# Pooled attention with a SoLU layer on one core: the first batch's scores in float32, q turned tile by tile on TensorE, and a new order of the program

## The chip, the core and the metric

The kernel runs on one core of one Trainium2 chip. What counts is the time of one execution on the device in microseconds (us). The engines are TensorE (PE in the profile; PEld is its weight load), VectorE (DVE), ScalarE (ACT), GpSimd (POOL) and SyncE (SP), which here only issues transfers. Each engine has its own queue and works through it in order; semaphores tie the queues together.

## The reference

```
B, H, S, D = 8, 8, 576, 64                          # q, k, v: float32
k_p = k.reshape(B, H, 72, 8, D).mean(axis=3)        # pooled by 8; v the same
scores = q @ k_p.T / sqrt(D)                        # per batch and head: 576 x 72
attn = softmax(scores)
x = (attn @ v_p)  -> (B * S, H * D) = (4608, 512)
h = x @ w_in                                        # 512 x 1024
solu = h * softmax(h)
ln = (solu - mean) / sqrt(var + 1e-06) * g_ln
out = ln @ w_out                                    # 1024 x 512
```

The weights lie in memory as 64-bit floats (4 MB each), so the kernel has to put float32 words together before it can use them.

## The kernel before

The 4608 tokens are cut into 36 tiles of 128 rows: four of a batch (rows 0 to 511), then one "mix" tile with the last 64 rows of two batches, then four of the next batch. A tile runs through scores (`scores`, L751, tile name `sc`), maximum and subtraction on VectorE (L762, L765), exponential on ScalarE (L772), sum, reciprocal and product on VectorE (L776 to L791, tile `e`), a split of `e` into two float16 parts (`e16`: ScalarE L813 and L815, GpSimd), a transposing DMA (`eT`), the product with v (`e_rest`, L841, tile `xp`), a split of x (`xT`: L849 on ScalarE, L853 on VectorE), the first layer (`mm1`, L873, tile `hp`, 24 matmuls of 512 columns), SoLU and norm on all engines, and the second layer (`op`, L1005).

A product of float32 is done as three passes over float16 parts, high times high and the two mixed ones. So scores need q and k in high and low parts. For q that is a maximum over the batch (`amx_q`, L348), a spread over the partitions on PE (`gq`), a power-of-two scale from it (L370 to L382), the high part (`q_hi`, L722, ScalarE), the low part (`q_lo`, L727, VectorE), and a transposing DMA on SP's queue (`q_T`, L739, tile `qT`). For the first batch's k: GpSimd pools it in adds by halves (`pool_kv`, L329), ScalarE doubles it (`k_two`, L387), PE turns it (`k_T`, L396, tile `kTp`), ScalarE and VectorE make the parts (L412, L421).

Before `hp` of tile 0 can start, the four pieces of w_in must be ready, and this is a chain of its own. A piece is loaded (`w_load`; the raw tiles are `wo` for pieces 0 and 1, whose place it borrows, and `wir2`, `wir3`), its exponent field is brought into place (`w_exp`, L512, ScalarE; `u_wi`), words are joined on VectorE (L524, L545), the largest absolute value is taken (`w_abs`, L535, ScalarE; `ab_wi`), and from all four comes one scale (`g_wi`, L553 to L577). Only then follow, for each piece, the high part (`w_hi`, L645, ScalarE, 1024 columns), on PE the residue (`w_res`: two float32 matmuls L666 against a scaled identity `dg` made at L659, each followed by a subtraction L669; tile `res_wi`, in the two PSUM buffers of `ps_h` that `hp` uses as well), and the low part from it (`w_lo`, L675, ScalarE).

The order is not a scheduler's: `ORDER` is a table of operation numbers, the program is issued in that order (`tc.manual_schedule`), and so it sets the sequence of every engine's queue, SP's with its loads and transposing DMAs among them. Pools with a fixed number of buffers (`raw8` and `raw4` for raw loads, `ps_s`, `ps_x`, `ps_h` in PSUM) add waits.

## Time and profile before

| | |
|---|---|
| Median of 3 runs | 480.9 us (480.87 to 481.13) |
| Span of the profiled execution | 478.6 us |
| Busy: PE, DVE, ACT, POOL | 444.0, 341.3, 354.1, 349.8 us |
| Chain that ended last, by engine | PE 82%, DMA 6%, DVE 5%, ACT 4% |

The span is what the profile covers of its execution. The profiled execution's own time outside the profiler is not recorded, so the profile stands beside the timed runs by its span: 2.3 us less than their median. A line name such as L666 is a line of the kernel before; `x16` is a number of instructions; `<-` says what ended an engine's wait.

### The profile page before, as it was taken

To read this page: it belongs to the slowest core of one execution; us is meant where nothing else is said; L and a number is where in the kernel's file an instruction comes from. 1 tells how busy PE (TensorE), PEld (TensorE's weight loads), DVE (VectorE), ACT (ScalarE), POOL (GpSimd) and SP (SyncE) were. 2 spreads that over 40 slices of the span, in tenths; PEclk is the share of its full clock that TensorE was granted. 3 is DMA by queue.
4 is the path that set the end of the run, shared out by engine and by line. 5 is a ranking of instruction groups with operands and counts; after the bars stand their busy time and mean duration, and the time that the engine had idled before them with its cause. 6 is when DMAs were issued, how large, how long until landed. Compare 5 with 4: busy or idle time off the path is not lost.

```text
span 478.6 us, 9046 instructions
## 1 busy us (share of the span) xinstructions
PE 444.0 (93%) x3100; PEld 230.5 (48%) x3100; DVE 341.3 (71%) x835; ACT 354.1 (74%) x593; POOL 349.8 (73%) x489
## 2 busy tenths in 40 slices
PE   0177999999999999999999999999999999999996
PEld 0033544555455555555545554555545554545462
DVE  2989998599668876677668976787657887783620
ACT  1789999769876687767876698677766688766751
POOL 6256789968999987997989568996999538535340
PEclk9999999999999999999999999999999999999999
DMA  8999864999889889899878888889997648436351
GB/s 259 417 347 214 229 120 109 186 227 235 192 213 195 219 184 216 177 209 205 202 164 198 186 205 169 205 174 209 205 208 165 150 101 144 113 86 147 74 136 59
DMA packets 201390, 89.14 MB, mean 186 GB/s; under 512 B 177664, under 2 KB 186112, under 8 KB 200832
## 3 DMA queue, kind: packets, MB, share of 16 engines
q1 hardware_dynamic: 201344, 88.57, 78.9%
q8 instruction: 24, 0.39, 0.4%
q14 instruction: 22, 0.18, 0.1%
HBM read 36.70 MB, written 9.44 MB: 96 GB/s over the span
## 4 chain that ended last, share of the span: by engine, by line
PE 82%; DMA 6%; DVE 5%; ACT 4%; issue 1%; SPq 1%; POOL 0%; ACTq 0%; POOLq 0%
PE op L1005 36%; PE hp L873 36%; PE xp L841 6%; DMA qT<-q 4%; PE sc L751 3%; DMA qr<-in_q_dram 2%; DVE wo L677 1%; DVE m L883 1%; DMA zT<-z 1%; DVE u_wo L524 0%; ACT xT L849 0%; ACT osb L1013 0%; ACT q L722 0%; ACT sc L772 0%; ACT ab_wo L535 0%
## 5 line engine op out<-in xcount | busy, mean ns | idle before, releaser
L1005 PE MATMUL op<-wo,zT 128*128 128x512 f16 (+1 forms) x888 | 197.3, 373 | 1.2 <-DMA zT<-z 0.7
L873 PE MATMUL hp<-wi,xT 128*128 128x512 f16 x864 | 195.8, 379 | 2.6 <-ACT xT L849 2.6
L873 PEld LDWEIGHTS <-xT 128*128 128x128 f16 x864 | 82.7, 98 | 97.8 <-ACT xT L849 3.2
L1005 PEld LDWEIGHTS <-zT 128*128 128x128 f16 x888 | 84.4, 98 | 91.8 <-DMA zT<-z 1.7
L940 POOL TENSOR_TENSOR z<-z,z 128x512 f16<-128x512 f32 x71 | 82.2, 1168 | 43.3 <-ACT z L927 40.9
L883 DVE TENSOR_REDUCE m<-hp 128x1 f32<-128x1024 f32 x36 | 44.0, 1223 | 28.3 <-PE hp L873 28.2
L820 POOL TENSOR_TENSOR e<-e,e 128x512 f16<-128x512 f32 x36 | 41.6, 1156 | 22.2 <-ACT e L813 22.0
L329 POOL TENSOR_TENSOR vr<-vr 128x512 f32<-128x512 f32 (+3 forms) x48 | 48.1, 1006 | 13.3 <-DMA vr<-in_v_dram 12.7
L932 ACT ACTIVATE z<-z,sz 128x1024 f16<-128x1024 f32 x36 | 41.2, 1145 | 17.1 <-DVE z L918 16.9
L894 ACT ACTIVATE z<-hp,nb,Hb 128x1024 f32<-128x1024 f32 x32 | 38.3, 1198 | 15.2 <-DVE nb L886 14.2
L918 DVE SCALAR_TENSOR_TENSOR z<-hp,rs,z 128x1024 f32<-128x1024 f32 x36 | 46.1, 1280 | 3.4 <-ACT z L894 2.0
L329 POOL TENSOR_TENSOR kr<-kr 128x512 f32<-128x512 f32 (+3 forms) x48 | 42.2, 889 | 2.9 <-DMA kr<-in_k_dram 2.3
L762 DVE TENSOR_REDUCE mx<-sc 128x8 f32<-128x576 f32 x36 | 27.2, 754 | 23.6 <-PE sc L751 23.4
L927 ACT ACTIVATE z<-z,sz 128x1024 f32<-128x1024 f32 x36 | 41.1, 1143 | 0.7
L841 PEld LDWEIGHTS <-vb 128*128 128x128 f16 x640 | 35.3, 98 | 8.2 <-DMA eT<-e 0.4
L1013 ACT ACTIVATE osb<-op,f 128x512 f32<-128x512 f32 (+1 forms) x37 | 24.7, 666 | 19.2 <-PE op L1005 11.9
L841 PE MATMUL xp<-eT,vb 128*128 128x128 f16 (+1 forms) x640 | 38.2, 214 | 0.0
L953 ACT ACTIVATE junk<-z 128x1024 f16<-128x1024 f32 x36 | 37.7, 1047 | 0.2
L732 POOL TENSOR_TENSOR q<-qr,q 128x512 f16<-128x512 f32 x28 | 32.3, 1156 | 7.2 <-ACT q L722 7.2
L776 DVE TENSOR_REDUCE sc<-sc 128x8 f32<-128x576 f32 x36 | 27.4, 762 | 13.5 <-ACT sc L772 13.3
L849 ACT ACTIVATE xT<-xp 128x512 f16<-128x512 f32 x36 | 21.3, 591 | 16.0 <-PE xp L841 15.7
L853 DVE SCALAR_TENSOR_TENSOR xT<-xp,xT 128x512 f16<-128x512 f32 x36 | 24.5, 681 | 6.2 <-ACT xT L849 6.1
(232 smaller groups left out, 588.2 us busy)
## 6 DMA issues: line engine op xcount, KB each, us to landing
kr<-in_k_dram SPq DMA_DIRECT2D x16, 512.0 KB, 4.3
qr<-in_q_dram SPq DMA_DIRECT2D x16, 512.0 KB, 4.9
vr<-in_v_dram SPq DMA_DIRECT2D x16, 512.0 KB, 4.8
out_dram<-osb SPq DMA_DIRECT2D x31, 256.0 KB, 3.0
wor<-in_moe_w_out_dram SPq DMA_DIRECT2D x4, 1024.0 KB, 9.2
wo<-in_moe_w_in_dram SPq DMA_DIRECT2D x2, 1024.0 KB, 7.9
wir<-in_moe_w_in_dram SPq DMA_DIRECT2D x2, 1024.0 KB, 11.9
out_dram<-osb SPq DMA_DIRECT2D x10, 128.0 KB, 2.3
```

Of the source, the lines that this page charges most:

```text
L329: nc.gpsimd.tensor_tensor(out=dst, in0=src[:, :, :n], in1=src[:, :, n : 2 * n], op=ALU.add)
L820: nc.gpsimd.tensor_tensor(out=m[:, 1], in0=e_pair(i)[:, :, :P], in1=m[:, 0], op=ALU.subtract)
L841: nc.tensor.matmul(xp[:, c, lo:hi], lhsT=vb[b % 2][:, x, c].rearrange("p j d -> p (j d)"), rhs=eT[:, e, lo:hi], start=(n == 0), stop=(n == 3),
L873: nc.tensor.matmul(hp[:, f], lhsT=xT[:, xt, c], rhs=wi[:, wt, c, f * 512 : (f + 1) * 512], start=(part == 0 and n == 0), stop=(part == 2 a ...
L883: nc.vector.tensor_reduce(out=small(i, "m"), in_=tl[i]["hp"], axis=AX.XY, op=ALU.max)
L894: nc.scalar.activation(z, t["hp"], AF.Exp, bias=t["nb"], scale=hsc(i, 0), accum_out=small(i, "se"))
L918: nc.vector.scalar_tensor_tensor(out=t["z"], in0=t["hp"], scalar=t["rs"], in1=t["z"], op0=ALU.mult, op1=ALU.mult, accum_out=small(i, "sz"),)
L927: nc.scalar.activation(t["zf"], t["zf"], AF.Identity, bias=t["sz"], scale=-float(DFF))
L932: nc.scalar.activation(t["z16"][:, 0], t["zf"], AF.Identity, bias=t["sz"], scale=-float(DFF))
L940: eng.tensor_tensor(out=t["z16"][:, 1, fs], in0=t["zf"][:, fs], in1=t["z16"][:, 0, fs], op=ALU.subtract)
L953: nc.scalar.activation(junk, t["zf"], AF.Square, scale=DFF**-0.5, accum_out=small(i, "V"))
L1005: nc.tensor.matmul(op_, lhsT=zT[:, zt, c], rhs=wo[:, wt, c, cols(hf)], start=(part == 0 and n == 0), stop=(part == 2 and n == len(todo) - 1),)
```

## The change

The first four tiles (`FULL`) get their scores another way. q of batch 0 is loaded in four pieces, one per tile (`load_q0`, runs of 256 bytes). PE turns a piece by four float32 transposes into PSUM (`q_turn`), ScalarE copies it to SBUF in float32 (`q_keep`), and PE takes the scores as four float32 matmuls of 144 columns against `kd`, which holds the turned pooled k in float32 as blocks of two heads over 128 rows with zeros beside them (`k_zero` on VectorE, two copies `k_put` on ScalarE). So for these tiles maximum, scale, parts and transposing DMA of q fall away, and the exponential's scale is the constant 1/64 (`s_exp`). Batch 0's k is pooled by VectorE, not GpSimd. The float16 form of its k is still needed, by the mix tile, and is made later, in the way of the other batches. The scores of tiles 1 and 2 lie in `ps_h` (`ASIDE`), not in `ps_s`. The first loads of batch 1's k and v go to `raw4`. The whole order is new.

```
 ORDER = (
-    2, 0, 1, 12, 3, 4, 11, 50, 5, 6, 56, 57, 7, 53, 8, 58, 54, 13, 182, 51, 52, 9, 183, 55, 75, 65,
+    0, 52, 2, 58, 53, 59, 54, 60, 1, 55, 56, 57, 61, 69, 3, 189, 4, 13, 82, 11, 76, 12, 7, 5,
...
-        if b == 0:
+        if b < 2:
             return ("raw4", which, b, part)
...
+    def load_q0(eng, i):
+        if "q" not in bat[0]:
+            bat[0]["q"] = p2.tile([P, 4, H, D], F32, tag="qr", name="qr0")
+        rows = q[0, :, :SA, :].rearrange("h (p s) d -> s p h d", s=4)[i]
+        eng.dma_start(bat[0]["q"][:, i], rows)
...
-        nc.gpsimd.tensor_tensor(
-            out=dst, in0=src[:, :, :n], in1=src[:, :, n : 2 * n], op=ALU.add
-        )
+        eng = nc.vector if (b, which) == (0, "kr") else nc.gpsimd
+        eng.tensor_tensor(out=dst, in0=src[:, :, :n], in1=src[:, :, n : 2 * n], op=ALU.add)
...
+    def k_zero():
+        t = p2.tile([P, 2 * NC, P], F16, tag="eT", name="kd")
+        bat[0]["kd"] = t.rearrange("p c n -> p (c n)").bitcast(F32)[:, :NR]
+        nc.vector.memset(bat[0]["kd"], 0.0)
+
+    def k_put(j):
+        r_ = slice(64 * j, 64 * j + 64)
+        nc.scalar.activation(
+            bat[0]["kd"][r_].rearrange("p (c e r) -> p c e r", e=2, r=SP)[:, :, j],
+            bat[0]["kTp"][r_, :NR].rearrange("p (c e r) -> p c e r", e=2, r=SP)[:, :, j], AF.Copy,
+        )
...
-    DIRECT = (0, 1, 2, 3)
+    FULL = (0, 1, 2, 3)
+    ASIDE = (1, 2)
...
+    def q_turn(i):
+        t = ps_x.tile([P, HB, P], F32, tag="x", name=f"qTp{i}")
+        turned[i] = t
+        for c in range(HB):
+            nc.tensor.transpose(
+                t[:, c], bat[0]["q"][:, i, 2 * c : 2 * c + 2].rearrange("p h d -> p (h d)"), ident
+            )
+
+    def q_keep(i):
+        t = p2.tile([P, H, P], F16, tag="qT", name=f"qT{i}")
+        t = t.rearrange("p h n -> p (h n)").bitcast(F32).rearrange("p (c n) -> p c n", n=P)
+        nc.scalar.activation(t, turned[i], AF.Copy)
+        turned[i] = t
...
+        if i in FULL:
+            for c in range(HB):
+                nc.tensor.matmul(
+                    sc[:, c // 2, (c % 2) * PR : (c % 2 + 1) * PR], lhsT=turned[i][:, c],
+                    rhs=bat[0]["kd"][:, c * PR : (c + 1) * PR], start=True, stop=True,
+                )
+            return
...
-        nc.scalar.activation(sc, sc, AF.Exp, scale=grp["ct", q_key(i)])
+        ct = 1.0 / 64 if i in FULL else grp["ct", q_key(i)]
+        nc.scalar.activation(sc, sc, AF.Exp, scale=ct)
```

Three places of the order carry the argument. The first is SP's queue from the program's start. A row says the line, the tile that is written, the memory it is read from, and the shape. Before:

```order
L598 DMA g_sb_107<-in_moe_g_ln_dram 128x8x1
L305 DMA qr0_141<-in_q_dram 128x4x256 x2
L295 DMA vr0_2_144<-in_v_dram 16x2x512 x2
L501 DMA wo_89<-in_moe_w_in_dram 128x2048 x2
L501 DMA wir2_152<-in_moe_w_in_dram 128x2048
L501 DMA wir3_155<-in_moe_w_in_dram 128x2048
L501 DMA wor0_159<-in_moe_w_out_dram 128x2x1024
L292 DMA vr0_0_164<-in_v_dram 128x2x512
L739 DMA_TRANSPOSE qT0_208<-q16_0_195 128x8x128
L292 DMA vr0_1_216<-in_v_dram 128x2x512
L501 DMA wor3_219<-in_moe_w_out_dram 128x2x1024
L739 DMA_TRANSPOSE qT1_224<-q16_1_206 128x8x128
```

After, with the line numbers of the changed kernel:

```order
L321 DMA qr0_152<-in_q_dram 128x8x64 x2
L302 DMA vr0_2_160<-in_v_dram 16x2x512 x2
L299 DMA vr0_0_164<-in_v_dram 128x2x512
L299 DMA vr0_1_167<-in_v_dram 128x2x512
L516 DMA wo_89<-in_moe_w_in_dram 128x2048
L321 DMA qr0_152<-in_q_dram 128x8x64
L516 DMA wo_89<-in_moe_w_in_dram 128x2048
L516 DMA wir2_196<-in_moe_w_in_dram 128x2048
L516 DMA wir3_224<-in_moe_w_in_dram 128x2048
L321 DMA qr0_152<-in_q_dram 128x8x64
L516 DMA wor3_248<-in_moe_w_out_dram 128x2x1024
L516 DMA wor0_280<-in_moe_w_out_dram 128x2x1024
```

The transposing DMAs of q (`qT0`, `qT1`) are gone. v's two pieces `vr0_0` and `vr0_1` stand ahead of the four loads of w_in (`wo` twice, `wir2`, `wir3`), q's third piece among them, and `g_sb` has gone to a later place. Behind the rows shown follow three loads of batch 1's k, two of `qm0`, `wor1`, `wor2` and then `eT0`, the first transposing DMA on the queue; before, `eT0` stood behind `qT1`, `wor1`, `qm0`, `wor2`, the small last piece of batch 1's k, `qT2` and two small loads of v.

The second is ScalarE's queue between the weights' exponents and the first piece's high part, `w_hi`. Before:

```order
L535 ACTIVATE ab_wi1_231,bnd_wi_221<-u_wi1_214 128x1024
L512 ACTIVATE u_wi3_235<-wir3_155 128x1024
L535 ACTIVATE ab_wi2_237,bnd_wi_221<-u_wi2_228 128x1024
L535 ACTIVATE ab_wi3_241,bnd_wi_221<-u_wi3_235 128x1024
L512 ACTIVATE u_wo0_245<-wor0_159 128x1024
L722 ACTIVATE q16_2_264<-qr0_141,sq('b', 0)_178 128x8x64
L659 ACTIVATE dg_wi0_284<-ident_103,sw_wi_257 128x128
L645 ACTIVATE wi_88<-wir3_155,sw_wi_257 128x1024
```

After:

```order
L431 ACTIVATE vp_0_92<-vp_0_92,sv0_264 128x384
L849 ACTIVATE e16_1_97<-e1_269 128x2x32
L472 ACTIVATE vr_99<-vp_0_92 32x128
L550 ACTIVATE ab_wi3_294,bnd_wi_252<-u_wi3_261 128x1024
L847 ACTIVATE e16_1_97<-e1_269 128x512
L755 ACTIVATE qT3_304<-qTp3_299 128x512
L472 ACTIVATE vr_99<-vp_0_92 32x128
L849 ACTIVATE e16_0_96<-e0_240 128x2x32
L469 ACTIVATE v2_0_308<-vp_0_92 128x256
L849 ACTIVATE e16_1_97<-e1_269 128x2x32
L527 ACTIVATE u_wo0_337<-wor0_280 128x1024
L660 ACTIVATE wi_88<-wir2_196,sw_wi_330 128x1024
```

Between the last `ab_wi` (the maxima) and the first write to `wi_88` stood the exponents of w_out's first piece (`u_wo0`), a part of q and `dg`; now seven rows stand there, `u_wo0` among them and six of the split of `e`, of q's last copy and of v. `dg` now follows `w_hi`.

The third is PE's queue ahead of the first layer of tile 0. Before, matmul rows alone, and of each group the first (a residue has four rows, scores and `xp` 16):

```order
L357 MATMUL gv0_344<-identb_105,amx_v_101 128x128
L666 MATMUL res_wi0_346<-wo_89,dg_wi0_284 128x512
...
L666 MATMUL res_wi1_373<-wo_89,dg_wi0_284 128x512
...
L357 MATMUL gq('m', 0)_394<-identb_105,amx_q_102 128x128
...
L751 MATMUL sc2_407<-kT0_211,qT2_321 128x72
...
L666 MATMUL res_wi2_427<-wir2_152,dg_wi0_284 128x512
...
L841 MATMUL xp0_446<-eT0_368,vb_0_94 128x128
...
L873 MATMUL hp0_471<-wi_88,xT0_466 128x512
```

After:

```order
L369 MATMUL g_wi_320<-identb_105,g1_wi_297 128x128
L775 MATMUL sc3_344<-kd_150,qT3_304 128x144 x4
L681 MATMUL res_wi2_364<-wir2_196,dg_wi0_351 128x512
...
L369 MATMUL gq('m', 0)_375<-identb_105,amx_q_102 128x128
L681 MATMUL res_wi3_401<-wir3_224,dg_wi0_351 128x512
...
L369 MATMUL gk1_410<-identb_105,amx_k_100 128x128
L681 MATMUL res_wi1_413<-wo_89,dg_wi0_351 128x512
...
L875 MATMUL xp0_426<-eT0_394,vb_0_94 128x128
...
L681 MATMUL res_wi0_471<-wo_89,dg_wi0_351 128x512
...
L907 MATMUL hp0_476<-wi_88,xT0_458 128x512
```

The scores of tile 2 stood between residues, those of tile 3 behind the first 16 matmuls of `hp0`; now the scores of all four tiles stand ahead of the first residue. The residue of the piece that is last has moved behind `xp0`, directly ahead of `hp0`.

## Rows read from the trace of the kernel before

**Rows 1.** The trace in stretches; busy us by engine, granted clock, DMA share, GB/s
```profile
26.00:32.00 6.00, 5.78 (x23) 2.43 (x22) 5.43 (x15) 4.69 (x7) 4.80 (x6) 1.00 1.08 390
60.00:440.00 380.00, 378.44 (x2707) 196.31 (x2705) 283.02 (x696) 291.90 (x499) 304.82 (x415) 1.00 0.81 178
```

**Rows 2.** The chain of waits, first 60 us: shares by line
```profile
by line: DMA qT<-q 33.9%; DMA qr<-in_q_dram 12.8%; PE hp L873 8.9%; DVE u_wo L524 3.9%; ACT q L722 3.5%; issue 3.4%; ACT ab_wo L535 2.7%; DVE sc L765 2.4%; DVE mx L762 2.4%; ACT e L813 2.1%; DVE m L883 2.0%; DVE amx_q L348 2.0%; SPq L297 1.
```

**Rows 3.** The timeline, PE at the first layer of tiles 0 and 1
```profile
45.81 3.63 PE L873 MATMUL hp<-wi,xT 128*128 128x512 f16 x16 [1.48 <-ACT xT L849]
53.51 1.90 PE L873 MATMUL hp<-wi,xT 128*128 128x512 f16 x8 [0.81 <-ACT xT L849]
```

**Rows 4.** The timeline, the first work on k
```profile
10.29 0.86 POOL L329 TENSOR_TENSOR kp<-kr 128x128 f32<-128x128 f32 x2
11.19 0.74 ACT L387 ACTIVATE k<-kp 128x640 f32<-128x640 f32 x1 [9.11 <-POOL kp L329]
13.58 1.35 PE L396 MATMUL kTp<-ident,k 128*128 128x128 f32 x5
```

**Rows 5.** The timeline, ScalarE from the first q part on, and the first residue
```profile
14.07 0.72 ACT L722 ACTIVATE q<-qr,sq('b', 0)_178 128x512 f16<-128x512 f32 x1 [2.15 <-DVE sq('b', 0)_178 L382]
24.99 1.10 ACT L512 ACTIVATE u_wo<-wor 128x1024 f32<-128x1024 f32 x1
27.09 0.39 ACT L659 ACTIVATE dg_wi<-ident,sw_wi 128x128 f32<-128x128 f32 x1
27.38 1.20 ACT L645 ACTIVATE wi<-wir,sw_wi 128x1024 f16<-128x1024 f32 x1
27.53 2.07 PE L666 MATMUL res_wi<-wir,dg_wi 128*128 128x512 f32 x2
```

**Rows 6.** The timeline, three groups of PE matmuls
```profile
26.48 1.14 PE L751 MATMUL sc<-kT,qT 128*128 128x72 f16 x16 [0.21 <-DMA qT<-q]
32.51 0.68 PE L751 MATMUL sc<-kT,qT 128*128 128x72 f16 x16 [0.35 <-ACT wi L645]
36.57 1.06 PE L666 MATMUL res_wi<-wo,dg_wi 128*128 128x512 f32 x2
```

**Rows 7.** Groups by line and form, first 60 us: count, busy, mean ns, idle before
```profile
L772 ACT ACTIVATE sc<-sc,ct('b', 0)_203 128x576 f32<-128x576 f32 x4 | 2.8, 706 | 1.7 <-DVE sc L765 1.7
L813 ACT ACTIVATE e<-e 128x512 f16<-128x512 f32 x4 | 2.5, 621 | 0.0
L815 ACT ACTIVATE e<-e 128x64 f16<-128x64 f32 x8 | 1.9, 245 | 0.0
L849 ACT ACTIVATE xT<-xp 128x512 f16<-128x512 f32 x3 | 1.7, 583 | 0.0
L791 DVE TENSOR_TENSOR e<-sc,r 128x576 f32<-128x576 f32 x4 | 3.0, 748 | 0.0
```

**Rows 8.** The timeline, ScalarE from v's scaling to a low part
```profile
37.48 0.61 ACT L407 ACTIVATE vp<-vp,sv 128x384 f32<-128x384 f32 x1
39.10 1.00 ACT L675 ACTIVATE wi<-res_wi 128x1024 f16<-128x1024 f32 x1
```

**Rows 9.** k of batch 0, loads: issues (ns, first and last start) and landing
```profile
L297 SPq DMA_DIRECT2D kr<-in_k_dram x2: 455/516/576, 1.4 to 2.1; - x2
DMA to landing us min/median/max: 2.7/3.4/4.5
```

**Rows 10.** The load of `g_sb`, next on the queue: landing
```profile
DMA to landing us min/median/max: 5.7/5.7/5.7
```

**Rows 11.** q of the mix tile: issues and landing
```profile
L313 SPq DMA_DIRECT2D qm<-in_q_dram x2: 677/681/685, 27.4 to 28.1; - x2
DMA to landing us min/median/max: 8.0/8.2/8.4
```

**Rows 12.** w_in pieces 2 and 3: issues and landing
```profile
L501 SPq DMA_DIRECT2D wir<-in_moe_w_in_dram x2: 430/430/430, 8.3 to 8.8; - x2
DMA to landing us min/median/max: 10.9/11.9/12.8
```

More of the change, by code (lines that the diff above doesn't have):

```diff
@@ L301, in load_q @@
     def load_q(eng, b, part):
-        if part == 0:
+        if "q" not in bat[b]:
             bat[b]["q"] = p2.tile([P, H, 4, D], F32, tag="qr", name=f"qr{b}")
@@ L945, in z_T @@
         t = tl[i]
-        if x == 0:
+        if "zT" not in t:
             t["zT"] = p3.tile([P, 2, CO, P], F16, tag="zT", name=f"zT{i}")
@@ L1099, in pool @@
         prev = last_p.get((nm, b - 2), ())
+        eng, rate = ("dve", 1.2e-3) if (nm, b) == ("k", 0) else ("pool", 2.4e-3)
         for part, cols in ((0, 512), (1, 512), (2, 256 if nm == "k" else 512)):
@@ L1102, in pool @@
             for lvl in range(3):
-                n = op("pool", (cols >> lvl) * 2.4e-3 + 0.1, t + part + 1.1 * lvl, pool_kv, b, nm + "r", part, lvl, r=[rk],
+                n = op(eng, (cols >> lvl) * rate + 0.1, t + part + 1.1 * lvl, pool_kv, b, nm + "r", part, lvl, r=[rk],
                        u=[raw_key(b, nm + "r", part)], w=[(nm + "p", b)] if lvl == 2 else [], after=[n] + list(prev if lvl == 2 else ()))
@@ L1110, in prep_k @@
         pool(b, "k", t)
+        two = []
         if b == 0:
[L1112 to L1123 removed]
+            two = [op("act", 0.74, t + 2.0, k_two, b, r=[("kp", b)], w=[("k16", "two")])]
+            op("pe", 1.2, t + 2.8, k_T, b, r=[("k16", "two")], w=[("s", "k", b)])
+            n = op("dve", 0.45, t, k_zero, w=[("eT", "k")])
+            for j in range(2):
+                op("act", 0.42, t + 4.2, k_put, j, r=[("s", "k", b)], w=[("eT", "k")], after=[n])
+            t += 24.0
+        n = op("act", 0.45, t + 6.0, kv_ps, "k", b, r=[("kp", b), ("sk", b)], w=[("kps", b)], after=two)
+        n = op("act", 0.72, t + 6.5, k_hi, b, r=[("kps", b)], w=[("k16", b)])
+        last_p["k", b] = [
+            op("pool", 1.45, t + 7.3, k_lo, b, r=[("kps", b)], w=[("k16", b)], after=[n])
+        ]
+        turn(t + 8.2, 1280, k_Td, b, r=[("k16", b)], w=[("kT", b)])
     def prep_v(b, t):
@@ L1226 @@
     loads_kv(0, "kr", 0.0, 0.01)
-    for j in range(2):
-        load(0.1 + 0.01 * j, 1.9, load_q, 0, j, w=[("qp", 0, j)], u=[("qr", 0)])
+    for i in range(4):
+        load(0.1 + 0.01 * i, 0.95, load_q0, i, w=[("qp", 0, i)], u=[("qr", 0)])
     m = [load(0.2 + 0.1 * c, 3.5, w_load, "wi", c, w=[w_raw("wi", c), ("w", "wi", c)])
@@ L1284, in tile @@
         key = q_key(i)
-        n = op("act", 0.72, t(-3, 2.0), q_hi, i, r=src + [("sq", key)], w=K("q16"), u=hq)
-        op("dve" if i in DIRECT else "pool", 0.85, t(-3, 2.8), q_lo, i, r=src + [("sq", key)], w=K("q16"), u=hq,
-           after=[n])
-        turn(t(-3, 4.0), 1024, q_T, i, r=K("q16"), w=K("qT"))
-        op("pe", 0.52 * mul, t(-2, 5.3), scores, i, r=K("qT") + [("kT", b) for b in bs],
-           w=[("s", i)])
-        op("dve", 0.75, t(-2, 6.4), s_max, i, r=[("s", i)], w=K("mx"))
@@ new lines, in tile @@
+        if i in FULL:
+            op("pe", 1.15, t(-3, 3.0), q_turn, i, r=src, u=hq, w=[("x", "q", i)])
+            op("act", 0.62, t(-3, 4.0), q_keep, i, r=[("x", "q", i)], w=K("qT"))
+            op("pe", 1.5, t(-2, 5.3), scores, i, r=K("qT") + [("eT", "k")], w=[sk])
+        else:
+            n = op("act", 0.72, t(-3, 2.0), q_hi, i, r=src + [("sq", key)], w=K("q16"), u=hq)
+            op("pool", 0.85, t(-3, 2.8), q_lo, i, r=src + [("sq", key)], w=K("q16"), u=hq, after=[n])
+            turn(t(-3, 4.0), 1024, q_T, i, r=K("q16"), w=K("qT"))
+            op("pe", 0.52 * mul, t(-2, 5.3), scores, i, r=K("qT") + [("kT", b) for b in bs],
+               w=[sk])
```

81 lines of the change are left out of this document (28 added, 53 removed), and 269 rows, old and new, of the table ORDER.

## The prediction

> **What bounds the kernel now.** I read the stretches of the trace first. From 60 to 440 us PE is busy for 378.44 of 380 us [rows 1]: nothing to be had there, unless the new order puts a wait in. So the change lives in what comes before that. There the chain of waits is the next view: of the first 60 us a third is the transposing DMA of q and an eighth q's load [rows 2]. That looks like 20 us to be had, but a chain names the last link, not what would be last without it. A transposing DMA on SP's queue lies behind the loads of weights that were issued ahead of it, so its link is long; but next to it runs a second chain, the weights'. The first layer of tile 0 starts at 45.81 and tile 1's waits once more for 0.81 us at 53.51 [rows 3]. What the change gives is how far these two move, not the length of the link.
>
> The weights' chain on ScalarE: from 14.07, when it takes up q's first part, ScalarE runs on to the last maximum, which ends where `u_wo` begins, at 24.99; `dg` follows at 27.09, the first high part at 27.38, and PE's first residue at 27.53 [rows 5]. From there PE has 18.3 us of residues, scores, waits and one product with v until 45.81. I now write the new times of these steps in order.
>
> **First exponential.** K's second large piece is issued at 2.1 and lands 4.5 us later, at 6.6 [rows 9]. GpSimd's last add on k ends at 11.15, `k_two` starts at 11.19 and takes 0.74, the five turnings take 1.35 [rows 4]. VectorE has done no such add of k; its nearest row is the product on 576 values, 0.748 [rows 7], 1.3 ns a value, so the last piece's 896 values take 1.2: k pooled at 7.8, 3.3 earlier. Then `k_two` to 8.5 and the turnings to 9.9, on PE beside q's. The two copies into `kd` (288 values, 64 rows) lie between 0.245 for 64 values and 0.583 for 512 from PSUM [rows 7], by length 0.42 each: 10.7. Scores in float32 do not occur before. Lower bound: turnings of 128 columns at 0.27 each, so 1.2 for four of 144; upper: a float32 matmul of 512 columns (its two records together) took 2.07 at 27.53 [rows 5], by columns 0.58, so 2.3. I take 2.1, nearer to the matmul, since the copy ahead is in float32 too: 12.8. Maximum and subtraction at 0.75 each: first exponential at 14.3. ScalarE's chain so begins 0.2 later than before.
>
> **ScalarE's stretch.** 14.07 to 24.99 is 10.9. Gone from it: two high parts of q and one of k at about 0.72 [rows 5], 2.2. New in it: two exponentials (1.41), a copy of q as long as that of x (0.58), a split of `e` in three (0.62 + 2 x 0.245) [rows 7], and of v's four instructions, 1.62 in all [rows 8], the first two (0.9), 4.0 together. Net +1.8, less 0.5 since consecutive instructions of ScalarE overlap by about 0.1 in the rows (1.10 from 24.99 runs to 26.09, a pair at 27.09 and 27.38 overlaps by 0.1): 12.2. Last maximum at 26.5.
>
> From there to the residue the order now has seven rows: 0.62, 0.58, 0.3, 2 x 0.245, 0.42 and `u_wo0` 1.10 [rows 5, 7, 8], less overlap 2.9. The scale chain on VectorE and PE, which took 2.1 (24.99 to 27.09), lies beneath them, so they cost only 0.8 more than the wait that they fill; were they elsewhere, the residue would start at 30.0. So high part at 29.4, `dg` at 30.5, residue at 30.8, with 1.20 and 0.39 from the rows [rows 5]: **3.3 later than before** (27.53).
>
> **PE.** What pays for it is that PE then has no scores and no waits for q among its residues. The level of its clock matters here: the granted-clock column says 1.00 for 26 to 32 us [rows 1], but 16 equal matmuls take 1.14 at 26.48 and 0.68 at 32.51 [rows 6], so I read the level from durations: 1.2 GHz at first, 2.4 GHz from about 32.5, after PE had worked without a break from 26.48. A residue's half takes 1.06 at 36.57 [rows 6], 1.1 with its subtraction, so 2.2 a piece at the upper level and 4.3 at the lower. Now PE's steady work starts at 30.8; I let the rise come as late after it as before: 36.8. Then piece 2 ends at 35.1, piece 3 (after a spread of a column, as short as a turning, 0.3) at 38.2, piece 1 at 40.6, the product with v (16 matmuls, 1.05) at 41.7, piece 0 at 43.9: first layer **1.9 earlier**. `hp` takes the PSUM buffer of piece 1's residue, so ScalarE must have written that low part too. Its queue has eight instructions to there from the low part of piece 3 at 39.0, of 0.25 to 1.1 us by the same rows, 5.7 less overlap of 0.7: 44.0, level with PE.
>
> **After that** PE is full in both kernels. Tile 3's scores (0.68) no longer stand there, nor the wait of 0.81 at 53.51, since tile 1's `e` is made before 30; one more spread, 0.2, has moved in: 1.3 less.
>
> Span 478.6 - 1.9 - 1.3 = 475.4. The timed median lies 2.3 above the span: **477.7 us**.
>
> **Loads.** The bound of the ScalarE stretch may be w_in's last piece. Before, pieces 2 and 3 landed at 19.2 and 21.6 [rows 12], 2.4 us a MB. Now 1 MB of v is ahead (+2.4); `g_sb` (4-byte elements) is gone from ahead, which was issued at 2.6 and landed 5.7 later [rows 10], at 8.3, 1.7 behind k; of q 256 KB fewer stand ahead (-0.6). Q's runs are 256 bytes. The mix tile's q has such runs: its two 128 KB landed at 35.8 and 36.1 [rows 11], 0.3 apart, so 0.6 for a tile of 256 KB, as fast as w_in. I add 0 to 1.2 for three tiles ahead. The last piece lands between 21.4 and 22.9; ScalarE wants it at 22.2, so this costs 0 to 0.7, and I take 0. The page "DMA: Bandwidth & Descriptors" of the Trainium skill, section Specifications, asks for at least 512 bytes a transfer for full rate, and speaks against these loads; were each tile at half the rate of the rows (an estimate from that page), the weights would land some 2 us later and the forecast would be 479.
>
> **Other bounds.** Copies into `kd` at 0.75 each: +0.7. Adds of k at 1 or 1.6 ns: -0.3 to +0.3. Scores at the bounds: -0.9 to +0.2. Rise of the clock: each us that it comes later costs half a us until the first layer, since work goes on at half speed. Batch 0's k in float16 has 10 us more than it needs before the mix tile; `kd` takes one of the two buffers of `eT` until tile 3's scores, which come before `eT1` wants it. I put both at nothing; each would cost its lateness in full.
>
> **Rivals.**
>
> Clock late (slower). PE's work up to 30 us is now short groups with gaps; if these leave it at the lower level, and the residues, with ScalarE's high parts between, don't raise it, the first layer itself does. At 46 us: 43.9 + 4.6; never before it: 7.1 later. Times 482.3 to 484.8. For it speaks that the level was low at 27 in the rows with all that ran before; against it that it rose among the same residues. It decides from a rise at 45 on. The page "TensorE: Matmul & The Clock Gate", Part 1, has the low level as the default that activity releases; the rows agree (1.14, then 0.68).
>
> Clock early (faster). Transposes and float32 scores keep PE at work from 8 us on, so the rise may come at 33: 1.9 less, 475.8.
>
> ScalarE or loads the bound (no change). Late w_in 0.7, dear copies 0.7, longer copies of q from PSUM 0.6: all of it delays the residue, 479.7.
>
> `eT0` late. It stands behind 5 MB now: q's last tile 0.6, four pieces of w_out 9.6, k 2.8, `qm` 0.6 after w_in's 22.2, then itself about 1.2: 37. Wanted at 40.6, 41 at latest. If these loads go at 3.0 a MB and issue waits add 2, it lands at 42 or later; piece 0's residue and `hp` are queued behind the product with v on PE, so each us counts in full: 479 to 481.
>
> **Chances.** My forecast's case (476.8 to 479.4) 0.50; clock early 0.15; ScalarE or loads 0.15 (half of it faster); `eT0` late 0.10 (half no change, half slower); clock late 0.10. Timing of this kernel can tell some 0.2%, 1.0 us, from no change. So faster 0.72, same 0.13, slower 0.15. The range takes in the clock at 33 and `eT0` late, and leaves out the late clock: 475.4 to 481.3.
>
> **What would show it.** Right: first exponential near 14.3, ScalarE without gaps to 26.5, first residue near 30.8, four residues with no scores between, `hp` at 44, no wait at tile 1. Wrong: residues of 4.3 us to the end; `hp` waiting for a DMA (`eT0`); gaps on ScalarE ending on `wo` or `wir`; a wait on PE after 60 us, where the new order has been read only in part.

## The result and the profile after

| | before | after |
|---|---|---|
| Median of 6 runs | 480.88 us (480.51 to 481.13) | 484.83 us (482.39 to 486.4) |
| Span of the profiled execution | 478.6 us | 482.4 us |
| First layer of tile 0 starts | 45.81 [rows 3] | 46.82 |
| From there to the end of the span | 432.8 | 435.6 |

After to before: 1.0081 (1.0060 to 1.0102). The change made the kernel slower, by 4 us; the forecast was 3 us faster. Its runs spread over 4 us, those of before over 0.6.

The stretches first, the answer to [rows 1]. From 60 to 440 us PE now works 374.90 of 380 us, where it was 378.44: it idles 5.1 us there, not 1.6.

```profile
14.00:18.00 4.00, 4.00 (x18) 3.84 (x17) 1.41 (x2) 0.70 (x2) 3.77 (x6) 1.00 1.06 379
18.40:21.50 3.10, 0.66 (x4) 0.42 (x4) 3.03 (x7) 2.88 (x5) 0.44 (x1) 1.00 1.01 428
21.70:38.60 16.90, 9.78 (x28) 6.27 (x29) 16.45 (x39) 16.85 (x31) 8.25 (x12) 0.50 1.05 369
38.70:46.80 8.10, 8.10 (x38) 3.69 (x36) 6.97 (x18) 8.04 (x12) 6.10 (x9) 1.00 1.17 290
60.00:440.00 380.00, 374.90 (x2687) 194.26 (x2687) 279.55 (x684) 286.78 (x493) 296.67 (x408) 1.00 0.82 176
```

The granted clock is 0.50 from 21.7 to 38.6, the lower level (1.2 GHz), and 1.00 from 38.7 on, the upper (2.4 GHz). Ahead of that the column reads 1.00 throughout, and durations tell more, as they did in the prediction: four equal turnings of q take 1.11 us at 13.18, 0.66 at 19.38 and 1.09 at 26.61. So PE began at the lower level, was at the upper one by 19.38, having worked without a break from 13.18 to 18.4, and was back at the lower one after a stretch in which it worked 0.66 us of 3.1.

Then the start, step by step against the forecast. VectorE's timeline, the pooling of k, answers to [rows 4]:

```profile
8.20 1.15 DVE L343 TENSOR_TENSOR kr<-kr 128x512 f32<-128x512 f32 x2 [1.82 <-DMA kr<-in_k_dram]
9.38 0.29 DVE L343 TENSOR_TENSOR kp<-kr 128x128 f32<-128x128 f32 x1
```

The add on the second large piece starts at 8.20, when that piece has landed; the last add ends at 9.67. ScalarE's timeline, which answers to [rows 4, 5, 8]:

```profile
9.75 1.28 ACT L399 ACT_TABLE_LOAD   x1 [9.75 <-DVE kp L343]
11.04 0.74 ACT L399 ACTIVATE k<-kp 128x640 f32<-128x640 f32 x1
...
18.20 0.64 ACT L806 ACTIVATE sc<-sc 128x576 f32<-128x576 f32 x1 [3.28 <-DVE sc L798]
...
25.91 1.17 ACT L527 ACTIVATE u_wi<-wir 128x1024 f32<-128x1024 f32 x1
...
30.08 0.19 ACT L550 ACTIVATION_READ_ACCUMULATOR ab_wi<-u_wi 128x1 f32 x1
...
32.98 1.19 ACT L660 ACTIVATE wi<-wir,sw_wi 128x1024 f16<-128x1024 f32 x1
34.08 0.38 ACT L674 ACTIVATE dg_wi<-ident,sw_wi 128x128 f32<-128x128 f32 x1
```

A load of the activation table stands ahead of `k_two` for 1.28 us, and it waits for k (`[9.75 <-DVE kp]`). The first exponential is at 18.20, the last maximum ends at 30.27, the first high part starts at 32.98. Pieces 2 and 3 of w_in, to hold against [rows 12]:

```profile
L516 SPq DMA_DIRECT2D wir<-in_moe_w_in_dram x2: 582/794/1007, 12.6 to 13.7; - x2
DMA to landing us min/median/max: 10.5/11.2/11.9
```

The last one, issued at 13.7 and landed 11.9 later, was there at 25.6; ScalarE takes it up at 25.91.

PE's timeline, three of the four turnings of q, scores of tiles 0 and 1, first residue, first layer of tile 0, the waits at 60 and 66, and in the second piece the one at 138:

```profile
13.18 1.11 PE L748 MATMUL qTp<-ident,qr 128*128 128x128 f32 x4
14.16 4.17 PE L775 MATMUL sc<-kd,qT 128*128 128x144 f32 x16
...
19.38 0.66 PE L748 MATMUL qTp<-ident,qr 128*128 128x128 f32 x4 [0.99 <-DVE pk L382]
...
26.61 1.09 PE L748 MATMUL qTp<-ident,qr 128*128 128x128 f32 x4 [1.44 <-DMA qr<-in_q_dram]
...
34.52 2.07 PE L681 MATMUL res_wi<-wir,dg_wi 128*128 128x512 f32 x2 [0.90 <-ACT dg_wi L674]
...
46.82 1.89 PE L907 MATMUL hp<-wi,xT 128*128 128x512 f16 x8
...
60.12 0.68 PE L784 MATMUL sc<-kT,qT 128*64 128x72 f16 x31 [0.57 <-DMA kT<-k]
...
65.91 0.23 PE L369 MATMUL gv<-identb,amx_v 128*128 128x128 bf16 x1 [1.55 <-DVE amx_v L360]
```

```profile
135.88 1.89 PE L907 MATMUL hp<-wi,xT 128*128 128x512 f16 x8
138.75 1.05 PE L875 MATMUL xp<-eT,vb 128*128 128x128 f16 x16 [0.98 <-DMA eT<-e]
```

Tile 1's wait of 0.81 [rows 3] is gone, as forecast. In its place stand 0.57 at 60.12, 1.55 at 65.91, 0.98 at 138.75 and some smaller ones. The waits that the timeline lists from the first layer to the end sum to 5.54 us, before to 2.12: 3.4 more, less 0.7 for the scores of tile 3 that have gone, close to the 2.8 us by which that part is longer.

### The profile page after: what moved, and what is told of

Same layout as the page of the kernel before. It is cut to its first block, busy times and chain, and to the rows that moved or that the text cites. A ratio compares the mean times of both kernels' runs of the same rounds, so it can differ in the third digit from the quotient of the medians.

```text
span 482.4 us, 8995 instructions
## 1 busy us (share of the span) xinstructions
PE 452.4 (94%) x3082; PEld 237.7 (49%) x3082; DVE 337.9 (70%) x833; ACT 353.2 (73%) x596; POOL 344.6 (71%) x481
## 4 chain that ended last, share of the span: by engine, by line
PE 73%; DMA 9%; DVE 9%; ACT 4%; POOL 3%; issue 1%; SPq 0%; ACTq 0%; POOLq 0%; DVEq 0%
PE op L1039 33%; PE hp L907 31%; PE xp L875 6%; DMA kr<-in_k_dram 4%; DMA eT<-e 3%; PE sc L784 3%; DMA qT<-q 1%; DVE m L917 1%; DMA zT<-z 1%; DVE wor L560 1%; PE sc L775 1%; DVE z L952 1%; ACT z L966 1%; POOL kr L343 1%; ACT z L928 1%
## 5 line engine op out<-in xcount | busy, mean ns | idle before, releaser
L854 POOL TENSOR_TENSOR e<-e,e 128x512 f16<-128x512 f32 x36 | 42.7, 1187 | 27.6 <-ACT e L847 27.4
L966 ACT ACTIVATE z<-z,sz 128x1024 f16<-128x1024 f32 x36 | 41.2, 1144 | 16.9 <-DVE z L952 16.7
L343 POOL TENSOR_TENSOR kr<-kr 128x512 f32<-128x512 f32 (+3 forms) x42 | 35.8, 863 | 2.9 <-DMA kr<-in_k_dram 2.5
L883 ACT ACTIVATE xT<-xp 128x512 f16<-128x512 f32 x36 | 21.4, 593 | 16.4 <-PE xp L875 16.1
```

The costliest lines, as they stand in the source:

```text
L343: eng.tensor_tensor(out=dst, in0=src[:, :, :n], in1=src[:, :, n : 2 * n], op=ALU.add)
L854: nc.gpsimd.tensor_tensor(out=m[:, 1], in0=e_pair(i)[:, :, :P], in1=m[:, 0], op=ALU.subtract)
L966: nc.scalar.activation(t["z16"][:, 0], t["zf"], AF.Identity, bias=t["sz"], scale=-float(DFF))
```

## The experiments

Each kernel is the changed one with the edit named, unless said otherwise. Numbers in brackets behind a time are the ratio to the kernel before, with its interval. Five kernels with exactly the same program up to the first layer (the changed one, e4, e10, e12, e13) have their first residue at 32.58 to 34.52 and their first layer at 45.38 to 46.82; so a step of the start that moves by less than 2 us between two profiles can't be told from chance.

The theories. **Start:** the 1.28 us of the table load and the crowd of loads ahead of w_in cost the 3 us that the first layer came later than forecast. **Crowding:** behind the first layer VectorE and GpSimd have no room, and a tiny multiplication waits for GpSimd. **Order:** the new order of everything behind the first layer costs the rest; a part of it, formed after the halves of the order below had told nothing, is **loads**: large loads stand directly ahead of a transposing DMA.

### e1: the table loaded early

```diff
+    warm = const.tile([P, 1], F32, name="warm")
     with tc.manual_schedule():
+        nc.scalar.activation(warm, phalf, AF.Copy)
```

> Kernel after with one more tiny activation at the head of ScalarE's queue, so that the table load (9.75 to 11.04 in the trace of after, on the way from the pooled k to the doubled k) is done before k is there. Theory A, the chain through k sets the first residue: first exponential from 18.2 to 16.9, first residue from 34.5 to 33.2, first layer from 46.8 to 45.6, time 1.3 less, about 483.5. Theory B, the landing of w_in sets it: the first exponential is 1.3 earlier too, but ScalarE then shows gaps that end on w_in's loads, the residue stays at 34.2 or later, time within 0.3 of after.

Measured: 485.75 us (1.0113, 1.0064 to 1.0162). ScalarE's timeline of e1:

```profile
0.79 1.28 ACT L1437 ACT_TABLE_LOAD   x1 [0.79 <-PEq L1454]
...
15.79 0.64 ACT L806 ACTIVATE sc<-sc 128x576 f32<-128x576 f32 x1 [3.26 <-DVE sc L798]
...
24.19 1.14 ACT L527 ACTIVATE u_wi<-wir 128x1024 f32<-128x1024 f32 x1 [0.24 <-DMA wir<-in_moe_w_in_dram]
...
31.64 1.12 ACT L527 ACTIVATE u_wo<-wor 128x1024 f32<-128x1024 f32 x1 [1.33 <-DMA wor<-in_moe_w_out_dram]
```

The table now loads at 0.79 and the first exponential comes at 15.79, 2.4 earlier, of which 1.1 is that the last add of k began earlier here (at 8.32). But the same engine then waits for w_in's loads (here 0.24, and 0.56 one piece earlier) and 1.33 for w_out's first piece, and the residue starts at 34.19, where it was. The gain is lost in the next chain: the loads are as late as k was.

### e2, e3, e14: v out of the way of w_in

In e2, v's two large loads and their adds stand behind w_in's four loads; e3 is e2 with e1's early table.

```diff
+    for n in (81, 80, 79, 78, 77, 76, 12, 11):
+        order.remove(n)
+        order.insert(order.index(10) + 1, n)
```

> Kernel after with the two large loads of v's first batch behind the four loads of w_in instead of ahead. Theory A, the chain through k: w_in lands some 2.4 us earlier, but ScalarE takes it up no earlier than now (18.75), residue at 34.5, time as after, 484.8. Theory B, the landing of w_in: last maximum and residue 1.5 to 2.4 earlier, time about 483. A third case: v comes 8 us later and its scaling, which stands in ScalarE's queue ahead of the last maximum, holds up the weights: residue later than 34.5, time above 485.

> Both edits together, early table load and v behind w_in. If the chain through k and the landing of w_in were both late by about the same (each hides the other), each edit alone gives under 0.5 and both together 1.3: residue at 33.2, time about 483.3. If A alone holds, this is as the early table load alone; if B alone holds, as v behind w_in alone.

Measured: e2 489.21 us (1.0182, 1.0164 to 1.0200), e3 488.78 (1.0167, 1.0150 to 1.0184). ScalarE of e2:

```profile
29.78 1.06 ACT L550 ACTIVATE ab_wi<-u_wi 128x1024 bf16<-128x1024 f32 x1 [6.09 <-DVE u_wi L539]
```

VectorE waits 6.65 us at v's maximum for v to be pooled, and the weights' joins stand behind that in its queue; ScalarE waits 6.09 for them. The residue starts at 39.46. This says nothing for or against the loads, only that v's whole chain must move with them. e14 does that (v's adds, maximum, scaling and parts moved behind the weights' steps, and the early table):

> Kernel after with the early table load and the whole chain of batch 0's v later: its large loads behind w_in and q, its pooling behind the split of e, its maximum and scale behind the scale of w_in, its four instructions on ScalarE behind three of the high parts; the exponents of w_out's first piece behind them too. If w_in's bytes are the bound of the start, once k's chain and v's places in the queues don't hold it: exponents of w_in's last piece at 23 (25.9 in after), first residue at 31, first layer at 44.5, time 482. If what is taken out ahead only comes back between residue and first layer (v's parts for the first product, loads behind): residue at 31 to 32, but PE waits for the product with v, first layer at 46.5 or later, time as after.

Measured: 487.93 us (1.0157, 1.0116 to 1.0197). The last piece of w_in was taken up at 23.15, 2.8 earlier. Yet the residue is at 33.75 and the first layer at 51.20. ScalarE and PE of e14:

```profile
32.20 1.21 ACT L660 ACTIVATE wi<-wir,sw_wi 128x1024 f16<-128x1024 f32 x1 [3.73 <-DVE sw_wi L592]
```

```profile
40.95 0.23 PE L369 MATMUL gq('m', 0)_377<-identb,amx_q 128*128 128x128 bf16 x1 [2.45 <-DVE amx_q L360]
```

The wait has gone on, to VectorE's joins and scale and from there to the maximum of the mix tile's q. The clock adds to it: PE works 1.05 of the 3.3 us from 38.7 to 42.0, and from 42.1 to 45.4 the granted clock is 0.50, where half of a residue takes 1.91 us and not 1.06. So with w_in taken up 2.8 us earlier the residue comes 0.8 earlier at most: VectorE is next behind the loads.

### e5, e8: the new form of the scores

e5 loads q in runs of 1 KB in place of 256 bytes, and leaves out putting it into the right places, so that its first four tiles compute with a permuted q; e8 (with e7's edits, below) turns q by head, and takes scores as 8 matmuls of 72 columns over 64 rows.

> Kernel after with the four loads of q in runs of 1 KB instead of 256 bytes; the same bytes per load, but they land in other places, so the first four tiles compute with a permuted q. If the short runs slow the transfers beside and behind them: k's second large piece lands at about 6.6 instead of 8.2, w_in's last piece 1 to 2 us earlier than its 25.5, first exponential 1.5 earlier, residue at 33.0, time about 483.3. If it is only the bytes ahead (v's megabyte): k and w_in land within 0.3 of after, time as after, 484.8.

> All edits of the run before, and q loaded as in the kernel before, in runs of 1 KB (two loads of four heads), turned by PE in pieces of one head and two tiles, so that the scores are eight matmuls of 72 columns against the turned k without zeros. Correct q with long runs. If the short runs cost what the run with a permuted q showed (1.4 us at the residue), residue at 31.5, first layer at 44.2, time 481. If the 256 KB more of q ahead of w_in take that back (2.4 us a MB, 0.6) and the waits after the first layer grow: first layer at 45.0, time 482.5. Scores of a tile as float32 matmuls take 2.1 as now if columns count, 3 or more if each matmul has a fixed cost.

Measured: e5 483.26 us (1.0056, 1.0039 to 1.0074), residue at 33.16, first layer at 45.25: within 0.2 us of what the same start does from one profile to the next. Whether the short runs cost anything stays open. e8: 487.06 (1.0130, 1.0100 to 1.0161). Its scores of two tiles on PE:

```profile
13.14 6.32 PE L779 MATMUL sc<-kd,qT 64*128 64x72 f32 x32
```

6.32 us for 16 matmuls of 72 columns (two records each), 0.39 a matmul, against 4.17 for 8 of 144, 0.52 each, both at the lower level of the clock (four turnings take 1.11 us just ahead of each, at 12.10 in e8 and at 13.18 in the changed kernel, and 1.11 still at 20.51 in e8). Half the columns saved a quarter of a matmul's time, and there are twice as many of them, so spreading the keys over 128 rows is the better form of the two. The forecast's 2.1 a tile was right.

### e6, e7: w_out's piece that is wanted first, loaded first

Both have the early table and the loads of w_out's pieces 0 and 3 exchanged; e7 has e4's edit too.

```diff
-    order = ORDER
+    order = [{18: 15, 15: 18}.get(n, n) for n in ORDER]
```

> Kernel after with the early table load, and with the loads of w_out's pieces 0 and 3 changed in their places, so that piece 0, whose exponents stand in ScalarE's queue ahead of the first high part of w_in, comes first. With the table load alone the last maximum was 1.7 earlier than in after, and ScalarE then waited 1.33 us for this piece. If that load is what took the place of the table load: no such wait, residue at 32.9 instead of 34.2, first layer at 45.4, time 1.3 less than with the table load alone. If another wait takes its place again (the scale chain on VectorE ends near 30.9; the residues want the high parts): residue at 33.8 or later, time within 0.5 of it.

> The early table load, w_out's pieces 0 and 3 exchanged, and the scale of w_out as a product of tensors. If the waits before the first layer and those after it add: first layer at 45.4 and the wait for the maximum of v at 0.5 or less, time 482.3. If VectorE's queue holds PE after the first layer whatever comes before: an earlier first layer gives longer waits from 58 to 70 us, together over 2 us, and the time is that of the product of tensors alone, 483.8.

Measured: e6 484.87 us (1.0086, 1.0057 to 1.0114), e7 485.69 (1.0106, 1.0067 to 1.0146). The wait for `wor` is gone in both. The residue starts at 34.13 in e6 and at 33.29 in e7, and PE then waits for the mix tile's q, for whose load VectorE waits 2.38 and 1.52 (first layer at 49.01 and 47.32). PE of e7:

```profile
38.79 0.23 PE L369 MATMUL gq('m', 0)_377<-identb,amx_q 128*128 128x128 bf16 x1 [1.28 <-DVE amx_q L360]
...
44.14 1.05 PE L875 MATMUL xp<-eT,vb 128*128 128x128 f16 x16 [0.22 <-POOL vb L484]
```

### e4, e12: the crowding

In e4 the multiplication `sg_wo` is written as tensor by tensor, in e12 it goes to GpSimd and the spread of v's maximum (`gv`) goes behind the next tile's matmuls.

```diff
-        nc.vector.tensor_scalar(out=sg, in0=g_sb, scalar1=sw, scalar2=None, op0=ALU.mult)
+        nc.vector.tensor_tensor(out=sg, in0=g_sb, in1=sw.to_broadcast([P, CO]), op=ALU.mult)
```

> Kernel after with one VectorE instruction written in another form: the scale of w_out (128x8, a product with a column) as a product of two tensors instead of tensor_scalar. In the trace of after this instruction took 1.92 us at 59.73 (0.22 before) and ended when GpSimd's two instructions beside it had ended. Theory C, VectorE's full queue from 42 to 66 us sets when PE gets on, and this wait is a part of it: the instruction takes 0.3, the wait of 1.55 us on PE at 65.91 (for the maximum of v) falls to 0.5 (GpSimd's last add on v, ending at 64.17, then holds it), time 1.0 to 1.1 less, 483.8. Rival: the wait is for v's late load and GpSimd's adds alone: wait stays at 1.3 or more, time as after. The start of the first layer, 46.8, is the same in both.

> Kernel after with two edits for the wait on PE at 65.9: the scale of w_out (128x8), which took VectorE 1.9 us in both forms and ended both times with GpSimd's instruction beside it, is computed by GpSimd itself; and PE spreads the maximum of v behind the last eight matmuls of tile 2's first layer, not ahead. Theory C, VectorE's queue holds PE there: the low part of x for tile 2 ends 1.6 earlier relative to the first layer (18.3 us after its start in after), no wait of over 0.5 between 12 and 24 us after the first layer's start (2.4 in all in after), from the first layer to the end 433.5 to 434.3. Rival: GpSimd, which now does the work and pools v, holds it: waits of 1.5 or more stay, 434.8 to 435.6.

Measured: e4 483.62 us (1.0066, 1.0036 to 1.0097). The instruction on VectorE of e4, and GpSimd of e4 beside it:

```profile
58.58 1.86 DVE L643 TENSOR_TENSOR sg_wo<-g_sb,sw_wo 128x8 f32<-128x8 f32 x1
```

```profile
58.51 0.71 POOL L343 TENSOR_TENSOR vr<-vr 32x256 f32<-32x256 f32 x1
59.19 1.14 POOL L854 TENSOR_TENSOR e<-e,e 128x512 f16<-128x512 f32 x1
```

It takes 1.86 us in this form too and ends at 60.44, just behind GpSimd's add (60.33); the wait for `amx_v` is 1.50. So e4 did not take the long multiplication away. Chance did in others: the same instruction took 0.28 us in e13, 0.26 in e5 and 0.22 in e10, whose programs are the changed kernel's up to 70 us but for the places of q in e5. Their waits from 58 to 70 us sum to 1.35, 1.41 and 1.30, where the changed kernel and e4 have 2.39 and 2.38. e7 has e4's form and took 0.27, so the form is not what decides. e12: 484.55 us (1.0086, 1.0065 to 1.0107). PE of e12:

```profile
65.19 0.23 PE L369 MATMUL gv<-identb,amx_v 128*128 128x128 bf16 x1 [0.48 <-DVE amx_v L360]
66.05 1.05 PE L875 MATMUL xp<-eT,vb 128*128 128x128 f16 x16 [0.63 <-DVE pv L382]
68.44 0.69 PE L784 MATMUL sc<-kT,qT 128*128 128x72 f16 x16 [1.34 <-DMA qT<-q]
```

With the multiplication gone from VectorE the wait is shared out over `gv`, v's scaled part and a transposing DMA of q: 2.45 us in the three, not less than in the changed kernel (1.55 and 0.27). But e12 also gives GpSimd the work and moves `gv`, so it can't tell what the multiplication alone costs. What the profiles beside it say is that about 1 us of the waits there goes with the long form of this multiplication, and the rest, 1.3 us and more, stays without it.

### e9, e10, e11: half of each order

e9 has the new order up to the first layer and the order of before from there, e10 the same from tile 4 on; e11 is the kernel before with the new order from tile 4 on.

> Kernel after up to tile 0's first layer, with all operations from there on in the order of the kernel before. In eight profiles of kernels with the order of after, the time from the first layer's start to the end of the span was 434.8 to 435.6; before it was 432.8, though PE had 0.7 us more to do there (scores of tile 3). Theory D, the new order from the first layer on costs this (it asks for batch 1's k and v, and for the mix tile's scores, 13 to 19 us after the first layer instead of 35): first layer at 45.7 to 47.2, from there to the end 432.1 to 432.8 or less, no wait for kT or the maximum of v, span 478 to 480, time 480 to 481.5. Rival: the part after the first layer is late because its start is (loads and VectorE late by the same amount): the time from there to the end stays above 434.5.

> Kernel after up to the first layer of tile 3, with the order of the kernel before from tile 4's first layer on. The waits before 76 us (kT 0.6, maximum of v 1.5, 0.3) stay; those after it (0.3, 0.5, 1.0 for eT at 138 us and others) go if they come from the new order there. Theory D splits the 2.4 us: from the first layer to the end 433.7 to 434.3, time about 1 us less than after. If all of it lies before 76 us: 434.8 to 435.6 as in after. If all lies behind: 433.

> Kernel before up to the middle of tile 4's first layer, with the order of the kernel after from there on, and nothing else of the change. First layer at 45.8 as before. If the new order behind tile 4 has waits of its own (eT at 138 us and others): from the first layer to the end 433.8 instead of 432.8, time about 1 us more, 481.9. If these waits only follow from what happens earlier in the kernel after: 432.8 and time as before.

Measured: e9 483.65 us (1.0069, 1.0045 to 1.0093), 435.0 us from the first layer on. e10 491.72 (1.0234, 1.0198 to 1.0269), e11 499.63 (1.0400, 1.0357 to 1.0444). PE of e9:

```profile
78.41 5.34 PE L1014 MATMUL op<-wo,zT 128*128 128x512 f16 x24 [0.71 <-ACT osb L1022]
...
121.75 1.07 PE L850 MATMUL xp<-eT,vb 128*128 128x128 f16 x16 [0.81 <-DMA eT<-e]
```

The old order behind the new start loses as much as the new one, by waits of its own (4.49 us to the end; the rows are the largest for ScalarE and for a DMA). As I read it, it asks for things in another rhythm than this start delivers. e10 and e11 wait 10.1 and 16.2 us, the longest of it where the two orders meet (4.20 for `osb`, 6.19 for `eT`), and their granted clock is 0.50 for some us behind these waits (82.5 to 89 and 106 to 116), which costs more. Two orders can't be compared by cutting them in half; the theory of the order needs a smaller edit.

### e13: two loads moved, nothing else

The loads of parts of batch 3's k and q, 512 KB each, stand in the changed kernel directly ahead of the transposing DMA of `e` for tile 9; here they stand behind it.

```diff
-    order = ORDER
+    order = list(ORDER)
+    for n in (677, 579):
+        order.remove(n)
+        order.insert(order.index(748) + 1, n)
```

> Kernel after with two 512 KB loads (k's and q's of batch 3) behind the transposing DMA of e of tile 9 on SP's queue, not directly ahead of it. In all profiles with the order of after PE waited 0.6 to 2.4 us at about 138 us for the product with v of tile 9. If the loads ahead on the queue make its landing late (9.2 us from issue, against 3.5 as the median): this wait is 0.2 or less and the time from the first layer to the end 0.6 to 1.0 shorter. If the parts of e come late (GpSimd): the wait stays.

Measured: 481.82 us (1.0016, 1.0000 to 1.0032; 10 runs, 480.42 to 484.02). The tile `eT` from 118 to 135 us, its issues and landing, in the changed kernel and then in e13:

```profile
L865 SPq DMA_TRANSPOSE eT<-e x2: 1627/2580/3532, 117.9 to 129.4; - x2
DMA to landing us min/median/max: 3.6/6.4/9.2
```

```profile
L865 SPq DMA_TRANSPOSE eT<-e x2: 1607/2143/2679, 116.6 to 127.9; - x2
DMA to landing us min/median/max: 3.6/4.2/4.8
```

PE of e13 at that place:

```profile
134.35 1.89 PE L907 MATMUL hp<-wi,xT 128*128 128x512 f16 x8
136.08 1.06 PE L875 MATMUL xp<-eT,vb 128*128 128x128 f16 x16
```

The longest way of `eT` falls from 9.2 to 4.8 us and PE passes from the first layer to the product with v without a wait. That wait was 0.60 to 2.36 us, 1.42 in the mean, in all eleven profiles with this order at that place, and it is gone in all four with the two loads moved (e13 and, below, e15, e16, e17): **the two loads ahead of the transposing DMA make this wait.** From the first layer to the end e13 takes 432.75 us, the changed kernel 435.58. The intervals of the two ratios don't meet, and the medians lie 3.0 us apart. That the edit is worth all of that is not shown. Of the 2.8 us between the two profiles the wait is 1.0; another 1.0 lies from 58 to 70 us, ahead of anything that the edit touches, and goes with the multiplication (0.28 us in e13). e4, nine runs of what is nearly the changed kernel, has 483.62.

### e16, e17, e15: several at once

e17 is e13 with w_out's first piece and the mix tile's q loaded ahead of the others, and w_out's piece 3 behind the first transposing DMA of `e`; e16 is e17 with the early table; e15 joins e12, e13 and e14.

> The kernel of the run with the two loads later (481.8, first layer at 46.35, 432.75 from there to the end), with the early table load, w_out's piece 0 first of the four, the mix tile's q directly behind it, and w_out's piece 3 behind the first transposing DMA of e. If the waits that took the place of the table load were these loads (w_out's piece 0 at 31.6, the mix tile's q at 38.8 to 40.5, e at 44.0): residue at 33.0, no wait over 0.3 between residue and first layer, first layer at 45.2, time 480.6, level with the kernel before or better. If a further wait comes (exponents of w_out's piece 3, GpSimd's adds on batch 1's k): first layer at 46 or later, time 481.5 or more.

> The same without the early table load. If the table load is on the path once the loads are out of the way: first exponential 1.3 later than in the run beside it, residue 34.0 to 34.3, first layer 46.3, time 1.0 more than it. If w_in's landing bounds both: residue and time within 0.4 of the run beside it.

> The edits of the three runs before together. If they add: first layer at 44.5, from there to the end 433.0, span 477.5, time 479.3, 0.2% faster than the kernel before. If the start takes back or the waits after the first layer grow when it comes earlier: span 480 or more.

Measured: e16 483.42 us (1.0064, 1.0045 to 1.0084), e17 482.51 (1.0041, 1.0029 to 1.0053), e15 488.73 (1.0160, 1.0129 to 1.0192). e16 and e17 differ by the table load alone; their first exponentials are at 16.72 and 17.25, their residues at 33.68 and 33.34. The early table gives nothing as long as w_in lands when it does. In e15 the wait at 138 is gone again, and e14's cost stays: its time is no better than that of e14. No kernel here beat the one before; e13 is level with it.

## Why the prediction was wrong

The forecast's span was 475.4, the measured one 482.4: 2.9 us of the 7.0 lie ahead of the first layer (43.9 against 46.82), 4.1 behind it (431.5 against 435.6). Steps that fell:

- **"After that PE is full in both kernels ... 1.3 less."** This is the larger error. The 0.81 and the scores did go, but the new order put waits in, and I had read its first 60 us only and assumed the rest: from the first layer to the end PE waits 5.54 us, not 2.12. e13 shows one: two loads ahead of a transposing DMA that PE waits for, 0.98 us here. The other lies at 58 to 70 us, 2.39. The changed kernel asks for the spread of v's maximum of batch 1 at 65.9 and the mix tile's scores at 60.1, 19 and 13 us behind the first layer; the kernel before did both at about 81.6, 36 us behind it. That this haste makes the waits is argued and not shown. A full VectorE alone does not tell the two kernels apart: it is at work for 9.66 us of the 10 from 50 to 60, and for 9.65 in the kernel before. Of the 2.39 us about 1.0 goes with the multiplication that took 1.92 us.
- **"First exponential at 14.3."** It came at 18.20. Of the 3.9 us, 1.9 are k: its second large piece landed 6.2 after its issue, at about 8.2, not 4.5 after it at 6.6, and the adds took 1.47 in place of 1.2 (in the four other profiles of this start the last add began at 8.2 to 8.9, here at 9.38). Another 1.28 is the table load. In the kernel before it ran at the start of ScalarE's queue and cost nothing; here `k_two` waits for two engines, the load takes over the wait for VectorE, and so it starts when k is pooled. No step of mine had it, and the order shows it: the load stands there with VectorE's wait and the activation with GpSimd's. The rest, 0.7, is in small gaps between the steps.
- **"Loads ... between 21.4 and 22.9; I take 0."** The last piece of w_in landed at 25.6. From issue to landing it took 11.9 us, 0.9 less than before [rows 12]; but it was issued at 13.7, not at 8.8. My sum had counted megabytes and not when SP's queue would come to it. ScalarE took it up at 25.91 without a wait, so here k set the pace and w_in was 0.3 us from setting it. With e1, e16 and e17 this shows why an early table gives nothing. My rival "ScalarE or loads the bound" had the loads, though 2.7 us too early, and not the late k.

The steps that held, in durations: 4.17 for the scores of two tiles (forecast 2.1 each), 12.1 for ScalarE's stretch from 18.20 to 30.27 (12.2), 4.25 from there to the residue (4.3), 12.3 from residue to first layer (13.1), without a gap on PE. The granted clock was at the upper level 4.2 us after the residues began, where I had let it come 6.0 after: that gave the 0.8 less. The early clock of my rival did come, by 19.38, with the turnings and scores that I had named for it, but it was gone at 21.7, ahead of the residues. So the chain was right and began 3.9 us late. This profile is the latest of the five with the same start: their first layer is at 45.9 in the mean, level with the kernel before, 2.0 behind the forecast. The late clock was no rival, though the time came out at the end of its range (482.3 to 484.8): that is luck.

The rival of the late `eT0` was right in its landing, and the late residues hid it. The first transposing DMA of `e` in the changed kernel:

```profile
L865 SPq DMA_TRANSPOSE eT<-e x1: 6447/6447/6447, 32.2 to 32.2; - x1
DMA to landing us min/median/max: 10.6/10.6/10.6
```

It landed at 42.8 (at 41.2 to 42.1 in the other four profiles of this start), where my sum had 37 and that rival 42 or later. The product with v came at 43.49 and did not wait; had the residues been on time, PE would have wanted it at 40.6 to 41 and waited some 2 us, since SP was issuing the loads ahead of it until 32.1. An estimate from these rows: 42.8, the product's 1.05 and a residue's 2.2 give a first layer at 46.1, not 43.9. So a third thing ended at about the same time as k and w_in.

The chances were too sure, because the unread part of the order stood as one sentence under what would make the prediction wrong, and got no chance. It covered 420 of 480 us.

Open: what makes the same start vary by 2 us between executions (the last add of k starts at 8.2 to 9.4), whether runs of 256 bytes cost anything, how the waits at 58 to 70 us could be closed, what an edit that keeps the multiplication short would give, and why the median of e13 is 3 us lower where the wait that it removed was 1.4 in the mean.

## What to carry to other kernels

An order that is replaced must be read to its end, and first for the large loads that it puts directly ahead of a transposing DMA for which PE waits. When two or three chains end at the same time, a single edit can move one of them and show nothing in the time; follow the first step that did move to the wait that took its place, as in e1 and e14. And look at which instruction carries a wait: a table load in front of the first activation can stand on the path although it reads nothing. And before a cause is read from one profile, look at the same instruction in the others: a multiplication that took 1.92 us here took 0.3 or less in most.
